# Sparse attention and two gated layers on one core: queries and keys of a pair of heads split once in half the columns and spread by transfers

## The chip, the cores and the metric

One core of a Trainium2 chip runs the whole program. The metric is the device time in microseconds of one execution; the kernel before was timed in three runs. Five engines work side by side, each through a queue of its own in a fixed order: TensorE (PE, matrix products into PSUM), VectorE (DVE), ScalarE (ACT), GpSimd (POOL) and SyncE (SP), which issues the transfers. GpSimd can't reach PSUM.

## What is computed

```python
def _attn_ref(q, k, v, tau):                     # each (4, 8, 576, 64)
    scores = scale * np.matmul(q, k.transpose(0, 1, 3, 2))
    thresh = np.max(scores, axis=-1, keepdims=True) - tau
    scores = np.where(scores >= thresh, scores, -1000000000.0)
    scores = scores - np.max(scores, axis=-1, keepdims=True)
    attn = np.exp(scores)
    attn = attn / (np.sum(attn, axis=-1, keepdims=True) + 1e-09)
    return np.matmul(attn, v)
x = attention, rearranged to (2304, 512)
x = (sigmoid(x @ w_gate) * (x @ w_val)) @ w_out  # inner width 1536
h = x @ w_in;  out = (h * cos(h)) @ w_out2       # inner width 2048
```

Everything is float32. The products run in a 32-bit format that keeps fewer bits, so each operand is split: a *high* part, rounded by a copy, and a *low* part, the value less the high part. A product is then made of high x high, high x low and low x high.

## The kernel before

There are 32 heads in 16 pairs (`Pair`, p = 0 to 15), four pairs to a batch. A pair has nine tiles of 128 query rows (`Queries`): four for each head's first 512 rows, and one (`h is None`) for the last 64 rows of both heads. A tile goes through PE (scores, L909, into one of two score banks `s`), DVE (row extreme, L915), ACT (exponent, L920), a threshold on ACT, DVE or POOL (L768 to L772), DVE (mask and sum, L923) and PE (transposes, L939 and L946). ACT then takes the high part of the transposed tile (L851) and its low part is made in one of three ways (`LOWS`, `LOWS_L`): by DVE (V, L862), by POOL from a copy of ACT's (G, L866 and L871), or by a product of PE's that subtracts the high part in the bank (T, L855 and L858). `Values` forms the products with the values (L1006), ACT and DVE add their halves into x32 (L976, L981), the row sums are inverted, sent through DRAM and spread (L1083, L1086), and x32 is scaled (L1097), split (L1115, L1119) and stored.

For a score, the 128 rows of a product hold the 64 columns of a head twice. `qh` holds the query highs in both halves of the rows, `ql` the query lows in both; `kk` holds the key highs in rows 0 to 63 and the key lows in rows 64 to 127. So qh x kk gives two of the terms and ql x kk the third (and a term low x low). For that, `Pair.load` fetches each of q and k twice, once into either half of the rows (two transfers of 64 rows; 1152 columns for q, 1216 for k, both heads side by side). Then the queries are scaled in place (letter s), the highs are taken (Q, J) and the lows (q on 128 rows, j on rows 64 to 127). `top_keys` and `last_queries` (letters k and d) copy what the tile of the last rows needs into `kh` and `qd`. The first pair is loaded and split in five pieces so that the first tile can start early (`begin` in `Pair.tasks`).

PE also runs a part of the feed-forward layer between attention's work: the gate and value products of batches 0 to 2 for three of the six column groups (letter P, L563 to L565, 144 groups of three matrices). A P needs the split x of two or four pairs of its batch. Their weights come as words that DVE shifts and joins (letters 4 and 5, L516 and L519; both operands in SBUF) before they are split.

Two things keep PE's clock up: 42 transposes of the identity into `warm` at the start (L597), and `filler` (letter D, L777), four transposes after certain scores (`FILL`), written into columns of the score bank that the scores leave free.

The order on each engine is written out by hand: one string for each engine in `ORDER`, a letter for each task, and which of the tasks with that letter comes next follows from the order in which they were made. `WHERE` names the engine of a pair's tasks (Q, q, J, j for queries and keys; Z, z for values; s for the scaling; X, x for the split of x; U for the scaling of x), `YS` that of a tile's threshold, `SHARED` the form of a value product. The rest of the program is put out after these strings and is ordered by `LATER` (L1877); PE goes from one to the other in its queue.

Of the kernel before, what the change touches and what calls it, by code (L numbers as in the profile page):

```python
# [9 lines left out]
F32 = mybir.dt.float32  # L10
# [45 lines left out]
        "SDDSTDSDDDDSTStNnTSNTSDtnDTTSNNNStTDNStTSTVDDtNSSTVBTtSSTTDDNtVSSTTVNNtSTVtSNnSTTNVtSNSBTtSNSTnVTTVNtSnSTTNN"  # L56
        "SNtPTPtPSSPVTTPSVPtSTPSBPPtTPSTSPTPStVPTTSSPVNtPNSPTSVtPTTPStVPTPBSPTtPSTPSTtPVSTTVtSSVTtVnSTTPSPtPTPPBSStPP"
        "TPSTSVtTPSPSTTVPtSPTSVtTVTStPSPPTBPStSTPVTTPSStVTPTPSPtSPTPStPVTTSVPtTPBSPStTPPTSPPTStVTPSStTVPSPSVTtVSPTTPP"
        "tSSTPBPtTSSTTVtPSTTVStSTtVnVTSTPStPTPBSPtTPSPTVSSTtVPSSTTPPtPTSPStPTVTSPtSTBPPTPVStSPTPSPTtPSVTTSVtSPTPSVPTt"
        "PSStTVBPTPSSTtPVTPSStTVPTTPSPTPtSPTPVSPttSPTPBSPTVStTVSTTPSPtVTPSStPPTtPSSPTVPTTSSVtPTPSBPTPtSSPTPTPStPSVTTV"  # L60
        "tSSTVtPTTVtPSBTPSPPTStPSTTVStVTPSTPPStPPTPStSVTPTSPtSTVPTBPSTtSPtVTPSSVTTVPStPTPtPPTPTPtVPBBVV"
    ),
    ACT=(
        "JQJQEQHwEYEHEhOEHo6HOEhowEHHHOOOYEhhHEO6hpwCEEHYH6hOsHEERwhCHaaHHYEhE6OFwEHCHHEOOh6hEYHFhpwOoEHYEOYHh6OEREHw"
        "aOhFHCoY6EEHHFahwOoEHHHOOOhhEEH6wehEeFHCEp6HEYehFHERwYYEChHeeEH6HehEYYEFHCwHEYeEHOhOFhp6eHEYhFwCYHeHEh6FHREe"
        "HEYheHCYEhHEXFeHEHHFhhEQHhEYpoaFHCHhEeEHeREEhYCHeHeEEhHCFEeHHEHFphheCHEhHFEHhFCEEYRHheeECHEHHeFhCEYYEFHHHeQE"
        "YYhhEeHhYpeFHHCEFZhECeHREYHChEHeeEChYHYEHFeEYYHEHFhheEFHhEpFECHHheHEREhHCeHEHhFYeEHEHFHhhJHhEYFEoHFpHCEhYHeR"
        "EhHeYEEHeFEEhHFCHHHEEYehhpeHEheEHHFhHCYEeEReCHFEHhYEHhECeEFCHHHEFhHphECEFHhCehHEEFCRHHYYEEhFCHeYhHEEHHHFXsHe"
        "hEhHEepFhhEHeRCEHeEFYhCHEHHFCEheYEFCHhhEEYHeheHHEYEeFpHHCEhFEHReEHCheEEHHeheEEFHCHHhhFpHEhFCHHYhEeRFCHEECHhE"
        "eeHCHFhEFEHHHEehhYeEHChEEYFHHephHEEFHCRHChhYEEHeFEFHCFHHEhhEHYhCpeHHXhFeFbFX"  # L70
    ),
    DVE=(
        "jqjMqKqMLMKKM4MKY5KMLYMK4KM5MKllKMlM4Y5KKIMMYlLYKK4lMML5KKlMM4KA5MlKlKAM4M5KKlMIMYKK45MMAzKLKAM4YKM5MllKKLMM"
        "Yl4KA5MKLIKMlAMLKK4lM5KLMMLlKKAMM4K5lKAMlMLlK4A5ILKlMALYMKLKlMMlKLKMALKLMLAllMKLxKAMLMIlKKLMMKKMlLMKKlMAMKYL"
        "LKLAllMIMKlLAKlMAYMKKLMMYlKKLMMlAKKALLMLMKllMLlKALIMKYAlKMMKzlKMLMlKKLMMAKLKLAllMMYYKALlMYAIKKLlMMLKKlMMLKLl"
        "AMKLKLLllAMMLKAKMLAIMlKLKMLlMYKKLMMAKKlAMMLLLKKllMLIMlYKKLLlAMMKKMYMKLlAKMlMKKMALLYKAlMMlYYIKKAlMMlLYKKAzMML"
        "KKlMMAlLKKLLLAxMLlMKLYlKMYAIllKMMKLMKYlAKMYLAMlKKAMMYllKKLlLMMYLKKAMMLYYIKAlLMKYKMMlYYKLKMLlMKKALLMllAILYlAK"
        "MLlKMAMKKMlMYYKLAMKlKAMLLMLllKKMMlKKLLMAMlLIYKKAMMllYKKLMMAAKLLMAllKKlULILxlxAUAAUxx"
    ),
    POOL=(  # L80
        "YZYzJYjs7cYQqYJ7jG7QqZYGz7YcYGJ7jsQ7YUqZY7XxcUXxYsYG7YQq7GJjY7GscQZGYzJ7qG7UjGYZzYcsxYUXqYYJGYjZYYGzYscQGJYG"
        "YqUZGjYXGczGsUXxxqGGYJGjscGQqZzJjUYXYGYGcYxZUYXxjGYsQzqYYYcsQYqGJZGYzjGsYcYGGUQZGqYGJGjUYcGXxZzYQqJYGUjGGcsZ"
        "XxGQqUXGxzJsGjYYcGQqGYGYGGYZcJjYzYUGZYGGzUYYcGGXXRR"
    ),
    SP=(
        "100W21kkdd0W21sWsssk0kWdd1ssssW0rrssssWdkk2RRdWssssrrWRRk0kWssss12ddgWgg0ddssssWrgg1sssrsWggRRgkDk0ssss2dgrr"
        "ssssRRgggk21kd0gssssDDgkr1rdgssssRg2dRkggssss0grgdrRRsgsssD2ggdg1kkssss0rDrdg2ssssg1gdRRggD2kkdssssrr1RRssss"
        "kggk0dssssggg1rr0sRsgss2dRggdkkDD0ssgrdsskkssssd2rggR1Rssssrr2g0Rksssggks1DddgRssssd0grr2ggRkssssdggRk10dggr"
        "ssDssrgssssggkgd1kR2ssgssRDggDdrssssdk2rRRkgssssggrrssssRRDDDDggg"
# [5 lines left out]
    "VTTVTTTGT VGVTGTTTT TGVTTTVGV VGVVGTVGV VVGVVVVGV VGVGVVGVG VGVGVVVVG GGVGVVVGV "  # L95
    "VGVVVVVVG VVVGVVVVV GGVGGVGGV GVGVVVVVG VGVGGVVGV VGVVGVVGV GGVGVVGVV VGGVGVGVV "
).replace(" ", "")
LOWS_L = (
    "TTVV VVTV TTVV VVVV VVTV VVVV VVVV VVVV VVTV VVVV VVVV VVVV VVVV VVVV VVVV VVVV "
# [10 lines left out]
    "SS.. S..S .... .... S... .... .... .... .... .... .... .... .... .... .... .... "  # L110
# [3 lines left out]
    Q="APPPPPAPAPPPPPPP", q="DPPPPPPPPPPPPPPP", J="APPPPPPPPPAPPPPP", j="DPPPPPPPPPPPPPPP",  # L114
    Z="PPPPPPPAPPPPPPPP", z="PPDPPPPDPPPDPPPP", s="APAPPPPPPPPPPAPP", X="PPAPPPPPPAPPPPAA", x="PPPDPPPPPDPPDDDD", U="PPPPPPPPPPPPPPDP",
)

YS = (
    "PPAPDDPAP DADDAPPPA AADPAPDPP DPAAAPAAA PAADAAPPP APPPAPPPD PPDADPAAA AADAPAAAA "
    "DDDPPPAPP AAPADPPPA PDAPDAPPD DDPDAAAPP DDPADDADA DADDDDDPP DAPPDDPAP PAPDADPPA "  # L120
).replace(" ", "")

BITS = "DDDDDDDDDDDD"

FILL = (
    "223002001 200002000 000000000 000000000 000000000 000000000 000000000 000000000 "
# [334 lines left out]
def tile_kernel(ctx: ExitStack, tc: tile.TileContext, q, k, v, tau, w_gate, w_val, w_out, w_in2, w_out2, out):  # L461
# [28 lines left out]
    def f32(ap):  # L490
        return ap.bitcast(F32)
# [99 lines left out]
    for t in (qhs[0][:, S:QW], qhs[1][:, S:QW], qds[0], qds[1]):  # L591
        nc.gpsimd.memset(f32(t), 0.0)
# [1347 lines left out]
```

## Time and profile before

| | us |
|---|---|
| median of 3 runs | 1111.09 |
| lowest, highest | 1110.85, 1112.88 |
| the profiled execution | 1111.66 |
| its span, first to last instruction | 1109.9 |
| PE busy | 1076.6 (97%) |
| DVE busy | 926.6 (83%) |
| ACT busy | 766.7 (69%) |
| POOL busy | 597.3 (54%) |
| first product of the feed-forward part (letter P) | at 84.96 |
| last attention product ends, `LATER` begins on PE | at about 401.7 |

Shares over the whole span mix stages. The attention stage ends near 402 us, and inside it the time before the first P and the time after it have to be read apart. A wait is put down to the operand that came last.

### The profile page before, as it was taken

The page shows a single profiled execution, that of the slowest core. Times are in us where ns is not written, and L with a number is a line of the kernel's source. Part 1 is how long each engine was busy: PE and PEld are TensorE (multiplying, and loading weights), DVE is VectorE, ACT ScalarE, POOL GpSimd, SP SyncE. Part 2 cuts the span into 40 slices and gives each one's busy share as a digit, 9 for nine tenths or more (in the row PEclk, how much of TensorE's full clock was granted, in tenths as well). Part 3 has the DMA queues.
Part 4 walks back from the last instruction along what each step waited for, and adds up shares of the span by engine and source line. Part 5 has one row for each costly group of instructions (what it writes and reads, how often), then busy time and mean ns, then how long its engine had stood idle before and what let it go on. Part 6 is the DMA issues. An engine that isn't in the chain of part 4 may idle for free.

```text
span 1109.9 us, 17653 instructions
## 1 busy us (share of the span) xinstructions
PE 1076.6 (97%) x5816; PEld 917.4 (83%) x5816; DVE 926.6 (83%) x1631; ACT 766.7 (69%) x1507; POOL 597.3 (54%) x508
## 2 busy tenths in 40 slices
PE   6889999999999999999999999999999999999998
PEld 6768888888888878987888888888888888888886
DVE  6999998998998856887887655879788899889997
ACT  5889879888888855555654434357876767797774
POOL 4788878878886625432234442244244525445563
PEclk9999999999999999999999999999999999999999
DMA  6657675766666449898876645685444445457752
GB/s 184 158 154 217 193 211 167 199 181 187 182 188 182 125 163 313 303 322 293 292 259 219 200 172 197 219 254 209 157 169 168 152 152 190 173 207 240 279 211 85
DMA packets 88093, 225.53 MB, mean 203 GB/s; under 512 B 14410, under 2 KB 22722, under 8 KB 78274
## 3 DMA queue, kind: packets, MB, share of 16 engines
q1 hardware_dynamic: 87842, 224.08, 63.1%
q8 instruction: 46, 0.75, 0.3%
q10 hardware_dynamic: 160, 0.33, 0.1%
q14 instruction: 45, 0.37, 0.1%
HBM read 150.18 MB, written 59.84 MB: 189 GB/s over the span
## 4 chain that ended last, share of the span: by engine, by line
PE 51%; DVE 1%; DMA 1%; ACT 0%; issue 0%; ACTq 0%
PE h L1391 5%; PE h L1392 5%; PE h L1393 5%; PE h L1580 4%; PE h L1581 4%; PE h L1582 4%; PE o L1700 4%; PE o L1701 4%; PE o L1702 4%; PE o L564 3%; PE o L563 3%; PE o L565 3%; DMA early<-gd 1%; PE o L1791 1%; PE o L1790 1%; PE o L1792 1%
## 5 line engine op out<-in xcount | busy, mean ns | idle before, releaser
L1626 POOL TENSOR_TENSOR g<-raws,g 128x512 fp32r<-128x512 f32 x68 | 94.6, 1400 | 138.1 <-ACT g L1625 115.9
L915 DVE TENSOR_REDUCE sm<-s 128x1 f32<-128x576 f32 x144 | 106.1, 750 | 10.9 <-PE s L909 8.1
L923 DVE SCALAR_TENSOR_TENSOR p<-s,sm,p 128x576 f32<-128x576 f32 x128 | 102.6, 812 | 12.0 <-ACT p L920 7.6
L920 ACT ACTIVATE p<-s,sm 128x576 f32<-128x576 f32 x128 | 94.0, 742 | 15.3 <-DVE sm L915 10.6
L1391 PE MATMUL h<-x,w 128*128 128x256 f32 (+1 forms) x304 | 101.4, 333 | 0.0
L1392 PE MATMUL h<-x,w 128*128 128x256 f32 (+1 forms) x304 | 101.3, 333 | 0.0
L1393 PE MATMUL h<-x,w 128*128 128x256 f32 (+1 forms) x304 | 101.3, 333 | 0.0
L851 ACT ACTIVATE PT<-t 128x512 fp32r<-128x512 f32 (+1 forms) x160 | 86.2, 554 | 21.6 <-PE t L939 18.1
L909 PE MATMUL s<-kk,qh 128*128 128x288 f32 x320 | 92.0, 318 | 9.3 <-DVE p L923 7.8
L1006 PE MATMUL v<-PT,vn 128*128 128x320 f32 (+2 forms) x532 | 84.8, 303 | 3.2 <-DVE x L981 3.2
L1710 DVE TENSOR_TENSOR y<-o,y 128x512 f32<-128x512 f32 x120 | 78.7, 682 | 6.1 <-PE o L1702 5.8
L939 PE MATMUL t<-ident,p 128*128 128x128 f32 x512 | 76.3, 276 | 3.5 <-DVE PT L862 1.9
L1006 PEld LDWEIGHTS v<-PT,vn 128*128 128x128 f32 (+1 forms) x532 | 74.0, 187 | 5.6 <-DVE x L981 4.1
L871 POOL TENSOR_TENSOR PT<-praw,PT 128x512 fp32r<-128x512 f32 x48 | 64.1, 1336 | 26.5 <-ACT praw L866 15.6
L1700 PE MATMUL o<-g,w 128*128 128x512 f32 x196 | 76.7, 392 | 0.5 <-ACT o L1716 0.5
L1701 PE MATMUL o<-g,w 128*128 128x512 f32 x196 | 76.4, 390 | 0.0
L1702 PE MATMUL o<-g,w 128*128 128x512 f32 x196 | 76.3, 389 | 0.0
L909 PEld LDWEIGHTS s<-kk,qh 128*128 128x128 f32 x320 | 58.8, 189 | 21.1 <-DVE p L923 9.9
L1580 PE MATMUL h<-form,w 128*128 128x512 f32 x192 | 75.0, 390 | 0.5 <-ACT side L1549 0.5
L1581 PE MATMUL h<-form,w 128*128 128x512 f32 x192 | 74.8, 389 | 0.0
L1582 PE MATMUL h<-form,w 128*128 128x512 f32 x192 | 74.7, 389 | 0.0
L528 POOL TENSOR_TENSOR w<-wt,w 128x512 fp32r<-128x512 f32 x30 | 39.6, 1325 | 64.5 <-ACT w L524 64.4
(207 smaller groups left out, 3520.2 us busy)
## 6 DMA issues: line engine op xcount, KB each, us to landing
w<-wd SPq DMA_DIRECT2D x62, 1024.0 KB
wd<-stage SPq DMA_DIRECT2D x64, 512.0 KB
gd<-st SPq DMA_DIRECT2D x64, 256.0 KB
wraw<-in_moe_w_out_dram SPq DMA_DIRECT2D x28, 512.0 KB
raw_k<-in_k_dram SPq DMA_DIRECT2D x30, 304.0 KB
raw_q<-in_q_dram SPq DMA_DIRECT2D x30, 288.0 KB
wraw<-in_moe_w_in_dram SPq DMA_DIRECT2D x16, 512.0 KB
spare<-gd SPq DMA_DIRECT2D x7, 1024.0 KB
```

The costliest lines, as they stand in the source:

```text
L909: nc.tensor.matmul(s[:, half, 0:HALF], qq, keys[:, half * HALF:half * HALF + HALF], start=(i == 0), stop=(i == len(mms) - 1),)
L915: nc.vector.tensor_reduce(self.sm()[:, 0:1], self.s()[:, :, 0:HALF], axis=AX.XY, op=ALU.min)
L1006: nc.tensor.matmul(o, w, x, start=z == 0, stop=z == len(steps) - 1)
L1391: nc.tensor.matmul(o, w_hi, x(0, c), start=begin, stop=False, **late)
L1392: nc.tensor.matmul(o, w_hi, x(1, c), start=False, stop=False, **late)
L1393: nc.tensor.matmul(o, w_lo, x(0, c), start=False, stop=c == KC - 1, **late)
L1580: nc.tensor.matmul(ps(), of(0, c), hi, start=fresh and c == 0, stop=False, skip_group_check=True)
L1581: nc.tensor.matmul(ps(), of(0, c), lo, start=False, stop=False, skip_group_check=True)
L1582: nc.tensor.matmul(ps(), of(1, c), hi, start=False, stop=c == 1, skip_group_check=True)
L1700: nc.tensor.matmul(ps(), of(0, c), hi, start=begin, stop=False, skip_group_check=True)
L1701: nc.tensor.matmul(ps(), of(0, c), lo, start=False, stop=False, skip_group_check=True)
L1702: nc.tensor.matmul(ps(), of(1, c), hi, start=False, stop=True, skip_group_check=True)
```

## The change

Queries and keys of a pair after the first are fetched once: the first head's columns in rows 0 to 63, the second's in rows 64 to 127, so 128 rows of 576 columns for q and 640 for k. They are scaled and split there, into `qsplit`, `ql`, `khi` and `klo`. Ten transfers then spread them: four copy the query highs of each head into both halves of the rows of `qh` (`both_rows`, letter u), four put key highs and lows into the halves of `kk` (`keys`, letter y), two put each head's query lows into its own rows of `qz` (`low_queries`, letter d). `qz` is zero in the other head's rows, so the third term is now qz x khi, with the key highs of both heads in the rows as they were split. The number and shape of PE's score products stay. `kh`, `qd` and their copies go.

The first pair keeps its five pieces; its inputs land in x32 and in `bc` instead of tiles of their own, and POOL copies its key highs (`first_keys`, a new task with the letter J), which all scores of the pair now await.

The warm transposes (9 groups instead of 14) go into `warm`, which takes its place in the ring of the output banks `v`; the first product with the values waits for them. The first ones are 36 instead of 42. At the start POOL zeroes 64 x 576 four times in `qz` and once in `khi`, instead of two `qd`.

All five strings of `ORDER`, and `LOWS`, `LOWS_L`, `SHARED`, `WHERE`, `YS` and `FILL` are new. Tasks by letter, before and after: POOL G 48, 51; POOL Y 55, 62; DVE Y 39, 53; ACT Y 50, 29; N 20, 18; n 7, 3; DVE l 89, 93; DVE z 3, 1; SP k 32, 0; d 32, 30; u 0, 60; y 0, 60. The products P, V, S and T are as many as before.

```diff
@@ ORDER and the tables @@
...
 FILL = (
-    "223002001 200002000 000000000 ...
+    "421001001 000000000 000000000 ...
@@ buffers @@
-    qls = [at.tile([P, 2 * QW], F32R, tag=f"ql_{i}", name=f"ql_{i}") for i in range(2)]
-    qds = [at.tile([P, P], F32R, tag=f"qd_{i}", name=f"qd_{i}") for i in range(2)]
-    for t in (qhs[0][:, S:QW], qhs[1][:, S:QW], qds[0], qds[1]):
-        nc.gpsimd.memset(f32(t), 0.0)
+    qlz = [at.tile([P, 2 * S], F32R, tag=f"ql_{i}", name=f"ql_{i}") for i in range(2)]
+    for i in range(2):
+        for t in (qhs[i][:, S:QW], qlz[i][64:128, 0:S], qlz[i][0:64, S:2 * S]):
+            nc.gpsimd.memset(f32(t), 0.0)
...
-    for _ in range(42):
+    for _ in range(36):
         nc.tensor.transpose(warm[:, 0:P], ident, ident)
@@ class Pair @@
+        def first_keys(self, part):
+            raw = self.first_raw("k", part)
+            moves = [(slice(64, P), SL, 0, S)]
+            if part.start == 0:
+                moves = [(slice(0, 64), SL, 0, S), (slice(0, 64), 0, SM, SL), (slice(64, P), 0, S, SL)]
+            for r, to, of, n in moves:
+                nc.gpsimd.tensor_scalar(self.khi()[r, to:to + n], raw[r, of:of + n], 1.0, 0.0, op0=ALU.mult, op1=ALU.add)
...
+        def both_rows(self, h, i):
+            nc.sync.dma_start(f32(self.qb()[64 * i:64 * i + 64, QW * h:QW * h + S]), f32(self.qh()[64 * h:64 * h + 64]))
+
+        def keys(self, h, i):
+            of = (self.khi, self.klo)[i]()[64 * h:64 * h + 64, SL * (1 - h):]
+            nc.sync.dma_start(f32(self.kb()[64 * i:64 * i + 64, S * h:S * h + S + SL * h]), f32(of))
+
+        def low_queries(self, h):
+            r = slice(64 * h, 64 * h + 64)
+            nc.sync.dma_start(f32(self.qz()[r, S * h:S * h + S]), f32(self.ql()[r]))
...
+        def whole(self):
...
+            for nm, load, high, low, n in (("q", "0", "Q", "q", S), ("k", "1", "J", "j", S + SL)):
...
+            dup = [[task("SP", 0.47, "u", lambda h=h, i=i: self.both_rows(h, i), qh, uses=[self.qh, self.qb], moved=S // 2)
+                    for i in range(2)] for h in range(2)]
+            kks = [[task("SP", 0.47, "y", lambda h=h, i=i: self.keys(h, i), (kh, kl)[i], uses=[(self.khi, self.klo)[i], self.kb],
+                         moved=S // 2) for i in range(2)] for h in range(2)]
+            low = [task("SP", 0.47, "d", lambda h=h: self.low_queries(h), ql, uses=[self.qz, self.ql], moved=S // 2) for h in range(2)]
+            return [[*dup[h], *kks[h], low[h]] for h in range(2)], []
...
-    def filler(s):
+    spare = buf("v", lambda: warm, 2, any_order=True)
+    fills = []
+
+    def filler():
 
         for _ in range(4):
-            nc.tensor.transpose(s()[:, 1, HALF:HALF + P], ident, ident)
+            nc.tensor.transpose(spare()[:, 0:P], ident, ident)
@@ scores @@
             if h is None:
-                mms = [(pair.qb()[0][:, q0:q0 + P], kk[:, k0:k0 + S]) for q0, k0 in ((SM, 0), (S + SL, S + SL))]
-                mms.append((pair.qd(), pair.kh()))
+                mms = [(pair.qb()[:, q0:q0 + P], kk[:, k0:k0 + S]) for q0, k0 in ((SM, 0), (S + SL, S + SL))]
+                mms.append((pair.qz()[:, SM:SM + P], khi[:, SL:SL + S]))
             else:
-                q0 = (QW + SL) * h + P * self.j
-                mms = [(qq[:, q0:q0 + P], kk[:, S * h:S * h + S]) for qq in pair.qb()]
+                q0 = P * self.j
+                mms = [(pair.qb()[:, (QW + SL) * h + q0:(QW + SL) * h + q0 + P], kk[:, S * h:S * h + S]),
+                       (pair.qz()[:, (S + SL) * h + q0:(S + SL) * h + q0 + P], khi[:, SL * (1 - h):SL * (1 - h) + S])]
```

## Rows read from the trace of the kernel before

**Rows 1.** Page: busy us and share of the span of each engine

```profile
PE 1076.6 (97%) x5816; PEld 917.4 (83%) x5816; DVE 926.6 (83%) x1631; ACT 766.7 (69%) x1507; POOL 597.3 (54%) x508
```

**Rows 2.** Stretches: length, busy us by engine, granted clock, DMA share, GB/s

```profile
20.00:85.00 65.00, 52.70 (x345) 44.33 (x343) 60.76 (x110) 53.68 (x121) 54.09 (x47) 0.97 0.60 157
85.00:402.00 317.00, 309.27 (x2010) 270.89 (x2009) 287.75 (x640) 266.09 (x591) 248.74 (x234) 1.00 0.64 179
402.00:1110.00 708.00, 700.37 (x3372) 589.32 (x3370) 568.24 (x864) 438.12 (x782) 288.06 (x212) 1.00 0.63 219
```

**Rows 3.** Timeline of PE, first P: start, duration, engine, line, operation

```profile
84.96 0.48 PE L563 MATMUL m<-xs_a,w 128*128 128x512 f32 x1
```

**Rows 4.** Groups of POOL, 0 to 402 us: count | busy us, mean ns | idle before

```profile
L685 POOL TENSOR_TENSOR kk<-raw_k,kk 64x1216 fp32r<-64x1216 f32 x15 | 42.1, 2804 | 1.2
L685 POOL TENSOR_TENSOR ql<-raw_q,qh 128x1152 fp32r<-128x1152 f32 x15 | 40.8, 2717 | 0.6
...
L1097 POOL TENSOR_TENSOR x<-x,bc 128x576 f32<-128x576 f32 x14 | 20.0, 1426 | 2.8 <-DVE x L981 2.7
...
L670 POOL TENSOR_SCALAR kk<-raw_k 128x1216 fp32r<-128x1216 f32 x14 | 17.0, 1215 | 0.0
```

**Rows 5.** Timeline of DVE: shifts of weight words, held and free

```profile
22.06 2.12 DVE L519 SCALAR_TENSOR_TENSOR wt<-we,wt 128x512 uint32<-128x512 uint32 x1
...
27.86 0.42 DVE L516 TENSOR_SCALAR wt<-wraw 128x512 uint32<-128x512 uint32 x1
...
37.50 2.72 DVE L516 TENSOR_SCALAR wt<-wraw 128x512 uint32<-128x512 uint32 x1
...
57.54 0.67 DVE L519 SCALAR_TENSOR_TENSOR wt<-we,wt 128x512 uint32<-128x512 uint32 x1
...
117.85 2.02 DVE L516 TENSOR_SCALAR wt<-wraw 128x512 uint32<-128x512 uint32 x1
```

**Rows 6.** Timeline of POOL at the same time

```profile
37.15 2.79 POOL L685 TENSOR_TENSOR kk<-raw_k,kk 64x1216 fp32r<-64x1216 f32 x1
```

**Rows 7.** Groups of DVE, 0 to 402 us

```profile
L862 DVE TENSOR_TENSOR PT<-t,PT 128x512 fp32r<-128x512 f32 x68 | 46.4, 685 | 3.3 <-ACT PT L851 2.6
...
L1119 DVE TENSOR_TENSOR xs_a<-x,xs_a 128x512 fp32r<-128x512 f32 x4 | 6.3, 1583 | 0.0
L685 DVE TENSOR_TENSOR vn<-raw_v,vn 128x640 fp32r<-128x640 f32 x3 | 4.2, 1412 | 0.1
```

**Rows 8.** Waits of DVE, 0 to 20 us: waiter, released by: us, times, longest

```profile
DVE p L923 <- PE s L777: 1.5, 1, 1.5
...
DVE sm L915 <- PE s L777: 1.3, 1, 1.3
```

**Rows 9.** Timeline, the start

```profile
1.36 6.81 PE L597 MATMUL warm<-ident 128*128 128x128 f32 x42 [1.36 <-POOL halfpi L476]
...
5.15 0.74 ACT L668 ACTIVATE kk<-raw_k 128x640 fp32r<-128x640 f32 x1 [1.70 <-DMA raw_k<-in_k_dram]
...
7.92 0.38 PE L909 MATMUL s<-kk,qh 128*128 128x288 f32 x1
```

**Rows 10.** Timeline of PE; a stretch, columns of rows 2

```profile
42.69 0.40 PE L909 MATMUL s<-kk,qh 128*128 128x288 f32 x1 [2.40 <-DVE p L923]
...
44.00:48.00 4.00, 4.00 (x27) 3.96 (x25) 3.33 (x9) 2.36 (x5) 3.48 (x2) 0.69 0.80 196
```

**Rows 11.** DMA issues, one issue on SP's timeline, and a wait of SP's queue

```profile
kh<-kk SPq DMA_DIRECT2D x32, 144.0 KB
...
33.90 0.59 SPq L689 DMA_DIRECT2D kh<-kk  x1
...
SPq L1086 <- DMA rd<-rs: 5.2, 5, 1.8
```

**Rows 12.** Timeline: query lows of the second pair, its first scores

```profile
30.05 2.64 POOL L685 TENSOR_TENSOR ql<-raw_q,qh 128x1152 fp32r<-128x1152 f32 x1
...
34.80 0.37 PE L909 MATMUL s<-kk,qh 128*128 128x288 f32 x1 [0.96 <-DVE p L923]
```

More of the change, by code (lines that the diff above doesn't have):

```diff
@@ L640, in queries, with load @@
-        def queries(self, to, part):
-            n, head = part.stop - part.start, part.start // S
-            if n <= S:
-                begin = part.start + (QW - S) * head
-                return to[:, begin:begin + n]
-            return to.rearrange("p (a n) -> p a n", a=2)[:, :, 0:S]
-        def as_queries(self, part):
-            raw = self.raw["q"][:, part]
-            return raw if part.stop - part.start <= S else raw.rearrange("p (a n) -> p a n", a=2)
-        def scaled(self, part, engine):
-            raw = self.raw["q"][:, part]
+        def load(self, nm, part=None, queue=nc.sync):
+            src = self.src[nm][self.p]
+            if nm == "v" or self.p:
+                self.raw[nm] = at.tile([P, src.shape[1]], F32, tag=f"raw_{nm}", name=f"raw_{nm}")
+                queue.dma_start(self.raw[nm], src)
+                return
+            src = self.src[nm][NP].rearrange("(d a) n -> d (a n)", a=2)
+            for i in range(2):
+                queue.dma_start(self.first_raw(nm, part)[64 * i:64 * i + 64], src[:, part])
@@ L708, in tasks @@
-            order = [(nm, i) for i in range(2) for nm in "qkv" if i < len(parts[nm])]
-            if begin:
-                order = [("q", 0), ("k", 0), ("q", 2), ("k", 1), ("q", 1), ("v", 0)]
-                nc.sync.dma_start(taus[:, 0:1], tau.to_broadcast([P, 1]))
-                self.load("q", parts["q"][0])
-                self.load("k", parts["k"][0], nc.scalar)
-                nc.scalar.activation(one, halfpi, AF.Exp)
-                nc.vector.tensor_scalar(factor_q, taus[:, 0:1], 0.0, scale, op0=ALU.is_ge, op1=ALU.mult)
-                nc.vector.tensor_scalar(off, taus[:, 0:1], 0.0, None, op0=ALU.max)
@@ L753, in tasks @@
+            self.vb = buf("vn", size=2)
+            of, rest = self.whole() if p else self.begin()
             self.scores = {(h, j): of[h] + rest * (j > 0 and h == 0) for h in range(2) for j in range(4)}
-            self.scores[None, None] = of[0] + of[1] + rest + keys + last_q
+            self.scores[None, None] = of[0] + of[1] + rest
     N = NP * NT
@@ L959, in __init__ @@
             pv = task("PE", products(n, (14 if self.shared else 9) + self.close), "V", self.product, *pair.ready[blk, h],
[L960 removed]
+                      *lasts, pair.v_done, pvs[0], *(fills if pvs[0] is None else []), uses=[bank, self.PT, self.LZ, pair.vb])
             pvs[0] = pv
@@ L1887, in _two @@
     t = a.reshape(NP, 2, S, D).transpose(0, 1, 3, 2)
-    parts = [t[:, 0], t[:, 1, :, SM:], t[:, 1, :, :SM]] + [t[:, 1, :, SM:]] * again
-    return _np.concatenate(parts, axis=2)
+    last, most = t[..., SM:], t[..., :SM]
+    both = _np.concatenate([last, most, last], axis=3)
+    heads = [both[:, 0, :, 0 if again else SL:], both[:, 1, :, :S + again * SL]]
+    whole = _np.concatenate(heads, axis=1)
+    first = _np.concatenate([t[0, 0], both[0, 1, :, :S + again * SL], t[0, 0, :, :again * SL]], axis=1)
+    return _np.concatenate([whole, first.reshape(1, P, -1)], axis=0)
 def _values(a):
```

255 lines of the change are left out of this document (140 added, 115 removed).

## The prediction

> **What bounds the kernel now.** I read the page first, then the same engines by stretches, then the idle times of each engine with what ended them. The page shows TensorE (PE) busy for 97% of the span and VectorE (DVE) for 83% [rows 1]; that is an average over stages. Cut in three, it separates [rows 2]. From 20 to 85 us PE is busy 52.7 of 65 us and DVE 60.8: DVE sets the pace, ScalarE and GpSimd (53.7 and 54.1) are close behind. At 84.96 the first gate product of the feed-forward part starts [rows 3]; it is the work that fills PE's gaps, and it cannot start before two pairs of heads of batch 0 are finished and split. From 85 to 402 us PE is busy 309.3 of 317 us; from 402 on 700.4 of 708. So the end is set by two things in series: how soon the first pairs get through DVE, and then PE's own work. An edit that shortens DVE's way before 85 us moves all that follows. An edit on GpSimd or ScalarE counts only through that, and after 85 us there are 7.7 us of PE's idle time to win in all.
>
> The change sits in that frame. It touches the preparation of queries and keys (GpSimd work nearly throughout), the warm transposes, and every order. Nothing after 402 us is changed; that stage keeps its length.
>
> **Sum, step by step.** The profiled execution took 1111.66 us for a span of 1109.9; the median of the three is 1111.09, 0.6 lower. I sum against 1111.66 and take the 0.6 off at the end.
>
> *The split in half the columns.* Before, a pair after the first costs GpSimd 2.72 us for the query lows and 2.80 us for the key lows, and three one-input copies (scale, query highs, key highs) of about 1.2 us each (40 on GpSimd in all, of which one group stands) [rows 4]: 9.2 us. After it the lows have 576 and 640 columns: 1.43 us, which is what a two-input operation of 576 columns takes [rows 4], and 2.80 x 640/1216 = 1.48; the copies halve to 0.6. That is 4.7 us a pair, 4.5 less, some 67 us over 15 pairs, of which about 14 go back to GpSimd in the new division of work (three more 512-column lows, seven more thresholds, value lows). GpSimd is not the engine that is late, so none of this is a gain by itself.
>
> What it does for DVE is. DVE operations whose operands all lie in SBUF stop while GpSimd runs. The shifts of the weight words take 0.42 and 0.67 us when free; the one at 37.50 took 2.72, because GpSimd's key lows ran from 37.15 to 39.94 [rows 5, 6]. Seven of them were held by a 2.7 or 2.8 us operation, the first at 22.06 and the last at 117.85 [rows 5]; together they lost 11.9 us, the five before 85 us 8.9 us. With operations half as long (1.45/2.76 = 0.53) and as many meetings the five lose 4.7, a gain of 4.2; if the chance of a meeting halves too, they lose 2.5, a gain of 6.4. I take 4.8, near the cautious end, since GpSimd gets other work in place. The two after 85 us (2.9 us) help only where PE waits: 0 to 1.5, I take 0.5.
>
> *What DVE gets instead.* I counted the letters of the old and new order lines of DVE up to the 36th row maximum (four pairs). The new one has three more 512-column lows at 0.685, two lows of x at 1.58, one value low less at 1.41 [rows 7], and small ones (two low strips more, two sums and a masking not yet reached) that cancel these down by about 1.4: 2.1 + 3.2 - 1.4 - 1.4 = 2.5 us more. Below, this may be 0, since the two x lows end on DVE sooner than behind GpSimd's queue and let the first products start earlier; above, the count up to the 45th maximum gives 5.8. I take +2.5. ScalarE has some 6 us less up to the same place and PE some 5 (warm transposes, and the subtractions by PE that were turned into lows on DVE); DVE covers both, so I put them at 0. If DVE were not late they would be worth up to those figures.
>
> *Warm transposes in a bank of their own.* Before, they write into the score bank, so the readers of the scores wait for them: DVE waited 1.3 and 1.5 us on them near the start [rows 8]. These waits go: 0 (another operand is late then) to -2.8. I take -1.5, because scores, maximum, exponent and mask form a chain in the first 20 us and no other engine covers it. There are 9 groups instead of 14. They now share the ring of the output banks, and the first output product waits for them; it needs the masks and transposes of the same tiles and comes later than they do, and that covers them.
>
> *Start.* The 42 first transposes run from 1.36 to 8.17 and the first scores at 7.92 come out of the same queue behind them [rows 9]. Six fewer give PE back 0.9 us. Against that the first scores now also need the keys copied by GpSimd: about 700 columns, at the rate of the 1216-column copy 0.7 us, after some 3100 columns of memsets at no more than that rate (3.1 us from 1.3 on). They start when the keys have landed, which is where ScalarE's copy starts at 5.15 [rows 9], and end near 5.9, beside the highs and lows of the same keys and before the 7.92. Without that cover, 0.7 us. I take 0; the ends are -0.9 and +0.7.
>
> *The clock.* After 2.40 us of idle PE before 42.69, which ended with a mask on DVE queued behind the held shifts, the granted clock falls; in 44 to 48 us it is 0.69 [rows 10], a mixture of 2.4 and 1.2 GHz, which takes 1.2 us of full speed from PE. A shorter hold makes that idle shorter; fewer warm transposes make another fall likelier. I take -0.7, with ends -1.2 and +1.2.
>
> *Transfers.* A pair now has two loads of 128 rows in place of four of 64 rows and twice the columns, and ten copies between SBUF rows in place of four: 60 for the query highs, 60 for the keys, 30 for the query lows, each of 64 rows and 144 to 160 KB like the one that they replace [rows 11]. By shape that is 22 MB of copies more, 4.7 and 9 MB of old copies and loads less: 8 MB net in 402 us, 21 GB/s on the 179 and 0.64 share of the DMA engines [rows 2], so a share near 0.72. SyncE issues one in 0.59 us [rows 11]. Queued ahead of use they cost nothing: the last of a pair's copies is issued up to 5 x 0.59 = 3 us after the split, and a transfer that depended on another waited 1.0 us on average and 1.8 at the longest [rows 11]. So 4 to 4.8 us are added behind a split that is 4.5 shorter, and the earlier start on GpSimd covers it. I take 0.
>
> The Trainium skill speaks against this edit: "SBUF — State Buffer", section "The DMA setup-cost knee", gives each transfer about 2 us whatever its size and asks for 128 rows and few large transfers, and the section before it says that 64 rows reach only half of the ports. By its figures one such copy is an estimated 2 + 147/218, or 2.7 us, and the copies of a pair would land 0.9 to 1.7 us later than by the rows. No row of this trace shows one transfer alone.
>
> Sum: -4.8 - 0.5 + 2.5 - 1.5 + 0 - 0.7 + 0 = -5.0, so 1106.7 for an execution like the profiled one and **1106.1 us** for the median. All good ends together give -12.8 (6.4, 1.5, 2.8, 0.9, 1.2), 1098.3; the bad ends 4.2 - 5.8 - 0.7 - 1.2 make +3.5, 1114.6, before any late transfer.
>
> **Rivals.** *Late transfers, slower.* The scores of a pair stand in PE's queue and wait for five copies that stand in SyncE's queue behind stores that themselves wait. For it: the old preparation is already just in time; the first query lows of the second pair end at 32.69 and its scores start at 34.80, 2.1 us later [rows 12]. Against it: GpSimd has more than 4 us a pair to begin sooner. The gain of 5.0 is gone at 0.33 us of waiting for each of 15 pairs; at 0.6 us it is 9 - 5 = +4, about 1115. The rule quoted above is this rival's.
>
> *Nothing to measure.* DVE stays 93% busy from 20 to 85 us, gets more lows and thresholds, and the time that it no longer loses to GpSimd is spent by other waits of an order written for a model. The 2.5 and 5.8 of added work against 4.2 to 4.8 of saved holds leave -0.5 or so: 1110.5. For it speaks that PE's 7.7 us after 85 are out of reach either way.
>
> *GpSimd was late as well, larger gain.* PE has 12.3 us idle from 20 to 85 us. If the freed GpSimd lets the pairs be prepared early enough that the first products begin 8 us sooner, and starts and warm transposes give 2.5 more, it is 1100. Against it speaks that DVE's idle time in that stretch is 4.2 us.
>
> **How the numbers follow.** About 0.2% (2.2 us) is what a measurement can tell from no change. The forecast, faster within 1102 to 1108.8, gets 0.50; the larger gain 0.12; nothing to measure 0.20; late transfers, or the clock falling again, 0.18. So faster 0.62, same 0.20, slower 0.18. The range goes from 1100 to 1113: below it lies half of the larger gain, above it most of the slower case.
>
> **What would show it.** In the profile after: no shift of the weight words near 2.7 us, and few above 1.5; no wait of DVE or ScalarE on a warm transpose; GpSimd some 50 us less busy up to 400 us; the first gate product 4 to 6 us before 84.96 and the stretch from it to the last attention product as long as before, 317 us. It is wrong if scores show waits on the copies, if the first product is no earlier, if the granted clock shows more low stretches, or if the stretch after the first product gets shorter, which would mean that it was not PE's own work.

## The result, and the profile after

| | before | after |
|---|---|---|
| median, us (4 runs each, side by side) | 1111.99 | 1091.93 |
| lowest, highest of after | | 1091.60, 1094.26 |
| profiled execution, us | 1111.66 | 1094.26 |
| first product of the feed-forward part (P) | 84.96 | 70.84 |
| last attention product ends | 401.7 | 384.95 |

The ratio of after to before is 0.9824, with a 95% interval of 0.9805 to 0.9843: 20 us faster, where 5 were forecast; 1091.9 lies below the range of 1100 to 1113. The profiled execution happens to be the highest of its four, so the traces have 17.4 of the 20 us to explain; the other 2.7 stand in no trace.

The first line is the page's busy time by engine of the kernel after, against [rows 1]:

```profile
PE 1071.8 (98%) x5784; PEld 912.5 (84%) x5784; DVE 909.9 (83%) x1647; ACT 764.4 (70%) x1488; POOL 543.7 (50%) x521
```

GpSimd is 53.6 us less busy; DVE is 16.7 us less busy although it has 16 instructions more. The stretches of the kernel after, cut at its own first P and at the end of attention (columns of [rows 2]):

```profile
0.00:70.84 70.84, 61.19 (x410) 53.05 (x410) 61.33 (x133) 59.59 (x127) 51.68 (x72) 1.00 0.79 215
...
70.84:384.95 314.11, 309.66 (x2005) 269.86 (x2003) 280.13 (x651) 266.06 (x581) 205.68 (x238) 1.00 0.74 206
384.95:1092.50 707.55, 700.95 (x3373) 589.62 (x3372) 568.45 (x864) 438.71 (x782) 286.35 (x212) 1.00 0.63 218
```

Before [rows 2, 3] the three lengths were 84.96, 316.7 and 708.2 us. So 14.1 us are gained ahead of the first P, 2.6 between it and the end of attention, and 0.6 behind. In the middle stretch PE is as busy as before (309.7 against 309.3); only its idle time shrank, from 7.7 to 4.5. The granted clock is 1.00 in all three; the stretch at 0.69 of [rows 10] is gone.

For the first stretch the same view of the kernel before, up to its own first P:

```profile
0.00:84.96 84.96, 66.95 (x438) 57.17 (x439) 70.58 (x128) 62.48 (x135) 60.47 (x63) 0.98 0.62 163
```

DVE, which sets the pace here, was busy for 70.58 us and idle for 14.38 (84.96 less 70.58). After, it is busy for 61.33 and idle for 9.51. The 14.1 us are thus 9.2 of busy time and 4.9 of idle time, and the runs below show a cause of its own for each. The shifts of the weight words in the same stretch, as groups of DVE (count | busy us, mean ns | idle before), before and then after:

```profile
L519 DVE SCALAR_TENSOR_TENSOR wt<-we,wt 128x512 uint32<-128x512 uint32 x8 | 12.9, 1607 | 0.1
L516 DVE TENSOR_SCALAR wt<-wraw 128x512 uint32<-128x512 uint32 x8 | 8.0, 1000 | 0.0
```

```profile
L520 DVE SCALAR_TENSOR_TENSOR wt<-we,wt 128x512 uint32<-128x512 uint32 x7 | 6.0, 863 | 0.0
L517 DVE TENSOR_SCALAR wt<-wraw 128x512 uint32<-128x512 uint32 x7 | 3.2, 450 | 0.0
```

At the free durations of [rows 5], 0.67 and 0.42 us, the sixteen of before should take 8.7 us and took 20.9: 12.2 us were lost to holds. The fourteen of after should take 7.6 and took 9.2: 1.6 lost. So the holds gave 10.6 us, two shifts that moved behind the first P gave 1.1, and all other work of DVE grew from 49.7 to 52.1 us, by 2.4: -10.6 - 1.1 + 2.4 = -9.3. With the idle time (-4.9), the stretch behind the first P (-2.6) and the last one (-0.6) that makes the 17.4 us.

### The profile page after: what moved, and what is told of

It is laid out like the page before. It is cut to its first block, busy times and chain, and to the rows that moved or that the text cites. A ratio compares the mean times of both kernels' runs of the same rounds, so it can differ in the third digit from the quotient of the medians.

```text
span 1092.5 us, 17726 instructions
## 1 busy us (share of the span) xinstructions
PE 1071.8 (98%) x5784; PEld 912.5 (84%) x5784; DVE 909.9 (83%) x1647; ACT 764.4 (70%) x1488; POOL 543.7 (50%) x521
## 2 busy tenths in 40 slices
DMA packets 94494, 234.06 MB, mean 214 GB/s; under 512 B 13258, under 2 KB 21570, under 8 KB 84674
## 4 chain that ended last, share of the span: by engine, by line
PE 51%; DVE 2%; DMA 1%; ACT 1%; issue 0%; ACTq 0%
PE h L1441 5%; PE h L1442 5%; PE h L1443 5%; PE h L1630 4%; PE h L1631 4%; PE h L1632 4%; PE o L1750 4%; PE o L1751 4%; PE o L1752 4%; PE o L565 3%; PE o L566 3%; PE o L564 3%; DMA early<-gd 1%; PE o L1840 1%; PE o L1842 1%; PE o L1841 1%
## 5 line engine op out<-in xcount | busy, mean ns | idle before, releaser
L1056 PE MATMUL v<-PT,vn 128*128 128x256 f32 (+3 forms) x532 | 84.7, 302 | 0.2 <-ACT st L1214 0.2
L919 POOL TENSOR_TENSOR PT<-praw,PT 128x512 fp32r<-128x512 f32 x51 | 66.7, 1307 | 35.4 <-ACT praw L914 16.9
L959 PE MATMUL s<-khi,ql 128*128 128x288 f32 x288 | 81.0, 295 | 0.6 <-DVE ql L670 0.6
L1675 ACT ACTIVATE g<-raws 128x512 fp32r<-128x512 f32 x106 | 64.3, 624 | 13.1 <-DVE raws L1718 8.3
```

The costliest lines, as they stand in the source:

```text
L959: nc.tensor.matmul(s[:, half, 0:HALF], qq, keys[:, half * HALF:half * HALF + HALF], start=(i == 0), stop=(i == len(mms) - 1),)
L1056: nc.tensor.matmul(o, w, x, start=z == 0, stop=z == len(steps) - 1)
```

## Shorter lows and an own bank, each alone in the old order

Three kernels keep the old split and the old strings. In the first, GpSimd takes the query and key lows of every pair after the first on half the columns only; half of these lows are left out, and besides that only one memset is added at the start.

```diff
+                if self.p and engine == "POOL":
+                    part = slice(0, S)          # queries
...
+                if self.p and engine == "POOL":
+                    part = slice(0, S + SL)     # keys
```

> The kernel before, strings and all, but GpSimd's query and key lows of pairs 1 to 15 compute half of their columns (1152 to 576, 1216 to 640); the other half of the lows is left out, so the scores lack terms. Lighter GpSimd is enough (no new order needed): the shifts lose 4 to 6 us to GpSimd in place of 16.6, first gate product near 77, 1100 to 1105 us. Order needed as well: the time stays within 1107 to 1112 us, because what stands behind each operation in the old strings still comes at its old place.

Measured: 1101.78 us against 1111.71, ratio 0.9907 (0.9888 to 0.9927), 9.9 us faster. Its first stretch, then one shift and the key lows that hold it (timelines of DVE and GpSimd: start, duration):

```profile
0.00:79.66 79.66, 65.72 (x439) 56.14 (x439) 65.12 (x128) 62.20 (x135) 53.59 (x64) 1.00 0.67 174
```

```profile
36.53 1.50 DVE L516 TENSOR_SCALAR wt<-wraw 128x512 uint32<-128x512 uint32 x1
```

```profile
36.18 1.57 POOL L689 TENSOR_TENSOR kk<-raw_k,kk 64x640 fp32r<-64x640 f32 x1
```

It is the shift that took 2.72 us in [rows 5]. Then it ended 0.28 us behind the GpSimd operation of [rows 6] (40.22 and 39.94); now it ends 0.28 us behind one that is about half as long (38.03 and 37.75). DVE runs the same 128 instructions in 65.12 us instead of 70.58, and its idle time stays, 14.54 against 14.38. So shorter lows act on DVE's busy time alone. A GpSimd that was late is not the way as far as the waits show: up to 402 us of the kernel before, DVE and PE's products wait for GpSimd only at the very start (1.3 and 1.4 us). The shifts lose 6.2 us instead of 12.2 before the first P, which comes 5.3 us sooner; attention ends 8.8 us sooner (392.87), so 3.5 more are won behind the first P, where the shifts up to 200 us lose 1.2 us instead of 4.5. The clock is 1.00 in 44 to 48 us here too. In the kernel before it was down shortly ahead of that and into it (columns of [rows 2]):

```profile
43.00:46.50 3.50, 3.50 (x18) 3.44 (x17) 2.56 (x8) 2.21 (x4) 2.90 (x3) 0.51 0.94 242
```

So the 9.9 us include whatever that cost, at most 1.7 us of PE's work.

Not every meeting holds the shift. At 57.54 us [rows 5] it took its free 0.67 us in the kernel before, and GpSimd's operation at that moment was the longer one, with 2.11 us where its group has a mean of 1.34:

```profile
57.25 2.11 POOL L871 TENSOR_TENSOR PT<-praw,PT 128x512 fp32r<-128x512 f32 x1 [0.39 <-ACT praw L866]
```

In the second, the kernel before gets the own bank for its warm transposes and nothing else; only the ten groups that come before the first product with the values stay.

```diff
-    "223002001 200002000 000000000 ...
+    "223002001 000000000 000000000 ...
...
-            nc.tensor.transpose(s()[:, 1, HALF:HALF + P], ident, ident)
+            nc.tensor.transpose(spare()[:, 0:P], ident, ident)
```

> The kernel before, its warm transposes in a bank of their own; of the 14 later groups the four that stand behind the first product with the values are left out (the bank is handed on by then). The changed kernel lost 4.5 us when its groups went back to the score bank. If the bank is worth that in any order: 1106 to 1108 us, the waits on the warm transposes in the first 20 us gone, first gate product near 81. If it is worth it only where the new order made room: 1110 to 1112; slower if the four groups that are missing let the clock fall.

Measured: 1107.10 us against 1110.61, ratio 0.9966 (0.9955 to 0.9977), 3.5 us faster. First P at 81.51:

```profile
0.00:81.51 81.51, 65.12 (x423) 55.02 (x423) 70.42 (x128) 62.30 (x135) 60.18 (x63) 0.98 0.66 170
```

Now the busy time stays (70.42 against 70.58) and the idle time falls from 14.38 to 11.09. The bank acts on DVE's idle time alone. The four groups that are left out have no part in it: they stood on PE behind the first product with the values, at 37.22 us in the kernel before, and the 3.45 us by which the first P comes sooner are there by 31 us (the same shift, before and then with the own bank):

```profile
30.77 2.48 DVE L519 SCALAR_TENSOR_TENSOR wt<-we,wt 128x512 uint32<-128x512 uint32 x1
```

```profile
27.32 2.92 DVE L498 SCALAR_TENSOR_TENSOR wt<-we,wt 128x512 uint32<-128x512 uint32 x1
```

What went is more than DVE's two waits of [rows 8]. In the first 20 us of the kernel before, ScalarE's exponent waited longer for the warm transposes, and they for DVE (us, times, longest):

```profile
ACT p L920 <- PE s L777: 3.7, 3, 1.8
...
PE s L777 <- DVE sm L915: 2.3, 3, 0.9
```

The third has both, and the scaling and the query highs on half the columns as well (these halves are left out).

```diff
+            part = slice(0, S)                  # scaling
...
+                if self.p:
+                    part = slice(0, S)          # query highs
```

> The kernel before, strings and all, with both: warm transposes in their own bank (the same ten groups) and GpSimd's and ScalarE's scaling, query highs, query lows and key lows of pairs 1 to 15 on half of the columns (the other half is left out, so the scores are wrong); key highs stay whole. No copies. That takes 4.0 of the 4.5 us a pair off GpSimd that the change takes off. If the gain is the lighter split and the bank, and the strings only follow it: 1093 to 1098 us. If the new strings carry a share of their own: 1100 us or more.

Measured: 1097.09 us against 1110.61, ratio 0.9880 (0.9865 to 0.9895), 13.5 us faster: the sum of the two, 9.9 + 3.5.

```profile
0.00:75.04 75.04, 64.17 (x423) 54.70 (x423) 64.12 (x128) 60.97 (x135) 52.09 (x65) 1.00 0.71 184
```

Busy 64.12, idle 10.92: both effects at once. The two add up, which leaves little for the shorter copies. From here to the kernel after 5 to 6 us are left (5.2 by the medians, 6.2 by the ratios). In the timelines up to 200 us, 9 of this kernel's 24 shifts are still held by a GpSimd operation (by over 0.15 us), and lose 6.6 us by it: query and key lows, but also a value low, probability lows (`PT`, L871 in the kernel before) and the scaling of x, which no split shortens. None of the nine is held mainly by a copy of key highs, the one operation that this kernel leaves long.

## The own bank in the new order

The kernel after with its warm transposes back in the score bank (the eighth of the nine groups goes with the ninth tile's scores instead of the sixth's).

```diff
-            nc.tensor.transpose(spare()[:, 0:P], ident, ident)
+            nc.tensor.transpose(s()[:, 1, HALF:HALF + P], ident, ident)
```

> The changed kernel with its nine later groups of warm transposes written into the score bank again, as before (one group of the sixth tile is moved to the ninth). If the bank of their own is worth what my prediction took, about 1.5 us, and at most 2.8: 1093 to 1095 us, DVE or ScalarE wait 2 to 5 us on them in the first 20 us. If it is worth nothing: 1092.

Measured: 1096.46 us against 1111.71, ratio 0.9868 (0.9849 to 0.9887): 4.5 us of the gain are gone, more than the 1 to 3 expected. Its stretches and its waits from 0 to 20 us (us, times, longest; L822 is the warm transpose there):

```profile
0.00:20.00 20.00, 14.96 (x85) 13.57 (x86) 8.16 (x16) 9.14 (x15) 9.37 (x23) 0.91 0.58 164
20.00:75.57 55.57, 47.74 (x326) 40.66 (x325) 52.39 (x118) 50.36 (x112) 42.82 (x49) 1.00 0.81 216
```

```profile
ACT PT L896 <- PE t L986: 3.3, 1, 3.3
DVE p L970 <- PE s L822: 2.9, 3, 1.3
...
PE s L822 <- DVE p L970: 2.0, 2, 1.0
...
ACT p L967 <- PE s L822: 1.6, 1, 1.6
```

Up to its first P DVE is busy for 60.55 us (after: 61.33) and idle for 15.02 (after: 9.51). Again only the idle time. The waits are not DVE's alone: ScalarE's exponent waits for the warm transposes, and the transposes, queued on PE behind the scores whose bank is in use, wait for DVE and ScalarE in turn. That is a ring through three engines, and pricing DVE's share of it gave too little. The clock of 0.91 in the first 20 us, where after has 1.00, has a share in the 4.5 us that this run doesn't divide from that of the waits.

## How much room GpSimd has in the new order

Three kernels change only the length of GpSimd's query and key lows in the kernel after. One writes each low twice in a single operation of 1152 or 1280 columns; one does it in two operations of 576 or 640; both do all the work, and some of it twice. The third takes half of the columns and leaves the other half out.

```diff
+            if nm != "v" and engine == "POOL":                         # one long operation
+                n = S if nm == "q" else S + SL
+                to = low_raw[nm].rearrange("p (a n) -> p a n", a=2)
+                raw, hi = (t.unsqueeze(1).to_broadcast([P, 2, n]) for t in (raw, f32(hi)))
+                eng.tensor_tensor(to, raw, hi, op=ALU.subtract)
+                return
             eng.tensor_tensor(to, raw, f32(hi), op=ALU.subtract)
```

> The changed kernel, but GpSimd's query and key lows of pairs 1 to 15 compute their columns twice in one instruction (2.8 and 3.1 us in place of 1.4 and 1.6; the second result lands on the raw input, which nobody reads again). Everything else as it was. Short operations: DVE is held again, shifts above 1 us on average, first gate product at 76 to 80, 1098 to 1104 us. Order: the strings place the shifts away from the lows, shifts stay below 0.8, at most 1094 us.

```diff
             eng.tensor_tensor(to, raw, f32(hi), op=ALU.subtract)
+            if nm != "v" and engine == "POOL":                         # two short ones
+                eng.tensor_tensor(raw.bitcast(F32R), raw, f32(hi), op=ALU.subtract)
```

> As the run with long lows, but the second result comes from a second instruction of the same size, so GpSimd has the same work in short pieces. Short operations: DVE can go between the two, so shifts stay near those of the changed kernel (0.44 and 0.78 us) and the time within 1092 to 1095 us. GpSimd late (its load counts, not the length of an instruction): the same time as with long lows, 1098 or more.

```diff
+            if nm != "v" and engine == "POOL":
+                n = (S if nm == "q" else S + SL) // 2
+                raw, hi, to = raw[:, 0:n], hi[:, 0:n], to[:, 0:n]
```

> The changed kernel with GpSimd's query and key lows of pairs 1 to 15 on half of their columns (288 and 320; the rest is left out). GpSimd still late in the new strings (doubled lows cost 20 us): 1085 to 1089 us. GpSimd has room now and PE's own work sets the pace from the first gate product on: within 1.5 us of 1092.

Measured: one long operation 1111.89 us against 1110.93, ratio 1.0013 (1.0002 to 1.0024); two short ones 1116.51, ratio 1.0050 (1.0033 to 1.0067); half 1089.24 against 1110.61, ratio 0.9806 (0.9792 to 0.9821). So the long lows give back all 20 us, far more than expected, and short ones of the same sum still more; halving the lows again brings only 2.7 us.

The waits of DVE that tell it are those for a threshold of GpSimd, up to 385 us in after and half, up to 450 in the other two (the order of the fences: after, long, two, half):

```profile
DVE p L973 <- POOL sm L815: 2.5, 3, 1.3
```

```profile
DVE p L984 <- POOL sm L826: 11.8, 12, 2.1
```

```profile
DVE p L980 <- POOL sm L822: 15.0, 13, 2.6
```

```profile
DVE p L980 <- POOL sm L822: 0.7, 2, 0.4
```

With one long operation the first P comes at 77.07, 6.2 us later than in after, and the shifts before it lose 7.6 us instead of 1.6: that is the hold. DVE's busy time grows by 5.6 of the 6.2 us there (66.97 against 61.33), of the threshold waits only 0.4 us fall there, and the granted clock of 0.96 can have cost no more than the rest. From there to the end of attention it takes 325.5 us instead of 314.1, 11.4 more, and there stand the threshold waits, 11.4 of the 11.8 us. PE's scores wait for those masks in turn, here up to 460 us in after and with one long operation:

```profile
PE s L959 <- DVE p L973: 2.5, 6, 0.7
```

```profile
PE s L970 <- DVE p L984: 13.5, 14, 2.3
```

So a long low does two things: it holds a shift, and it stands ahead of a threshold in GpSimd's queue, for which DVE's mask waits. Two short operations hold the shifts less (3.5 us lost before the first P) and delay the thresholds more; their first P comes at 75.93 with a granted clock of 0.93 before it. What of their longer time the clock costs, and what the waits, these runs do not divide.

## The split and the order apart

Can the order be had without the split, or the split without the order? The first kernel puts the old split under the new strings and tables, with the own bank (a few neighbouring letters exchanged where an operand had no buffer yet; `kh` gets a second buffer).

```diff
-ORDER, LOWS, LOWS_L, SHARED, WHERE, YS, FILL of before
+those of after; on SP no u, and k for the last two of each four y
```

> Queries and keys are split as before (full width, no spreading copies but those for the last tile), under the strings and tables of the changed kernel, with its 36 first and 9 later warm transposes in their own bank; SyncE's string has the spreading copies taken out, six tasks of pair 13 stand a few places later, and kh has two buffers. Short operations (the gain is DVE no longer held by 2.7 and 2.8 us operations of GpSimd): the holds come back, shifts of the weight words near 1.1 and 1.4 us, 1103 to 1110 us. Order (the strings and tables bring the gain, whatever the split): 1092 to 1097 us. Both needed: in between, near 1100.

Measured: 1156.28 us against 1110.93, ratio 1.0406 (1.0387 to 1.0425), 45 us slower than before, where 1092 to 1110 was expected. One wait of DVE and one of PE, up to 450 us:

```profile
DVE p L926 <- POOL sm L770: 31.0, 15, 8.4
```

```profile
PE s L912 <- DVE p L926: 18.5, 21, 2.8
```

The new strings hand GpSimd seven thresholds more, and behind the long split DVE's masks wait up to 8.4 us for one. In the kernel before no mask waits for a threshold of GpSimd.

The second puts the new split under the old strings and tables with warm transposes in the score bank, SyncE's order left to the program's planner; the third takes the new string for SyncE.

```diff
-ORDER, LOWS, LOWS_L, SHARED, WHERE, YS, FILL of after
+those of before, with JJ ahead on POOL; SP planned (second) or the string of after (third)
```

> The new split and its copies under the strings and tables of before, with 42 first transposes and 14 groups in the score bank; SyncE's tasks stand in the order in which the program's own model finds them ready. Short operations: shifts below 0.8 us on average, first gate product near 72, 1095 to 1100 us. Order: shifts still held about half as long as before, 1105 to 1111 us; slower than before if the copies come late in an order that has no room for them.

> As the run of the new split under the old strings, but SyncE follows the changed kernel's string (six of its tasks and one of ScalarE's stand a few places later). If the first such run was slow only because its SyncE string was bad at the start (the first weights came 7 us late): 1100 to 1107 us, first gate product near 78. If the old strings of the compute engines don't fit the new split: 1110 or more.

Measured: 1123.84 us against 1110.93, ratio 1.0117 (1.0097 to 1.0137), and 1226.67 against 1111.71, ratio 1.1039 (1.1017 to 1.1062). Waits of PE in the second:

```profile
PE t L896 <- ACT PT L892: 10.6, 4, 8.6
...
PE s L952 <- DMA qh<-qsplit: 1.8, 1, 1.8
```

And one of DVE, up to the first P:

```profile
DVE wt L513 <- DMA wraw<-in_moe_w_gate_dram: 7.0, 1, 7.0
```

The holds fall (the shifts up to 200 us lose 4.1 instead of 16.6), yet the time grows: DVE is busy for only 61.67 of the 97.33 us up to the first P, and 7.0 us of its idle time are one wait for the weights, whose load the planned order of SyncE brings late. The third shows only that a string of SyncE that fits no other string costs far more than the change is worth. Neither part alone is a gain as it stands in the change, copies and all: old and old 1111, old split and new order 1156, new split and old order 1124, new and new 1092. What the split takes off GpSimd is a gain in the old order too, as the half lows show; what costs more under the old strings these waits tell only in part.

## The copies

The first of two kernels issues each of a pair's ten copies twice in a row, to the same place; the second sends a further copy of the same rows to places of their own in DRAM, 150 transfers more.

```diff
+            for _ in range(2):
                 nc.sync.dma_start(f32(self.qb()[...]), f32(self.qh()[64 * h:64 * h + 64]))
```

> The changed kernel with each of the 150 spreading copies issued twice in a row (150 more transfers, 22 MB more, some 80 us more of SyncE's queue). Copies are hidden with room to spare: within 1 us of 1092. Copies are nearly late already (the rival of late transfers): scores wait for them, 1096 us or more.

```diff
+            nc.sync.dma_start(junk[self.p, 2 * h + i, :, 0:S], f32(self.qh()[64 * h:64 * h + 64]))
```

> The changed kernel with a second transfer behind each of the 150 spreading copies that takes the same rows to a place of its own in DRAM, so that it waits for none (in the run with doubled copies each second copy waited some 2.4 us in SyncE's queue for the first one to the same place). Copies hidden with room in DMA and in SyncE's queue: within 2 us of 1092. The DMA engines or SyncE's queue nearly full: 1097 us or more, with waits of PE on copies.

Measured: 1473.26 us against 1111.71, ratio 1.3255 (1.3229 to 1.3280), and 1167.87 against 1110.61, ratio 1.0514 (1.0494 to 1.0533). The first did not load the transfers as meant: the second copy waits in SyncE's queue until the first has landed, and all behind it waits too. That wait measures a copy. Waits of SyncE's queue:

```profile
SPq L714 <- DMA qh<-qsplit: 146.6, 60, 4.7
...
SPq L724 <- DMA ql<-ql: 73.3, 30, 4.4
SPq L719 <- DMA kk<-khi: 73.0, 30, 5.1
SPq L719 <- DMA kk<-klo: 67.3, 30, 4.0
```

360.2 us over 150 copies: 2.4 us from the end of an issue to the landing, at most 5.1. In the second nothing waits so; waits of SyncE up to 460 us are replaced by issues back to back, here on its timeline:

```profile
34.57 0.77 SPq L714 DMA_DIRECT2D qh<-qsplit  x1
35.38 0.71 SPq L715 DMA_DIRECT2D junk<-qsplit  x1
36.18 0.62 SPq L714 DMA_DIRECT2D qh<-qsplit  x1
36.84 0.69 SPq L715 DMA_DIRECT2D junk<-qsplit  x1
```

```profile
POOL raw_q L691 <- DMA raw_q<-in_q_dram: 20.6, 6, 7.7
POOL vn L706 <- DMA raw_v<-in_v_dram: 17.8, 5, 6.0
...
PE s L963 <- DMA kk<-klo: 8.4, 4, 2.8
```

Summed over SyncE's timeline (an issue together with the short gap to the next of its kind), after has 480 issues that fill 298 us of the 385 up to the end of attention, before 421 that fill 277 of 402; with the extra copies it is 630 that fill 407 of 459. Loads of the next pairs, queued behind the copies, then come late, and with them the split. In after PE, DVE and ScalarE wait for no copy at all, and GpSimd once, for 1.4 us. So the copies are hidden, but SyncE is 77% filled, 89% with the extra copies, and 150 transfers more cost 76 us. They also load the DMA engines (share 0.80 between the first P and the end of attention, 0.74 in after); the run doesn't divide the two.

## Why the prediction was wrong

**The frame held in the main.** The end is set by the first P and then by PE's own work: 14.1 of the 17.4 us lie ahead of the first P, and the stage behind attention kept its length to 0.6 us. No shift is near 2.7 us (the longest up to 200 us is 1.34), no wait on a warm transpose is left, and GpSimd is 53.6 us less busy, 51.9 of them before attention's end. But the first P is 14.1 us earlier, not 4 to 6, and the stretch behind it is 2.6 us shorter than the 317 us that it was to keep. The prediction named that as a sign of being wrong: PE's work there is the same, and the gain came out of the 7.7 us of idle time, of which its sum had taken 0.5.

**The held shifts, -4.8 and -0.5: the step that failed most.** The mechanism was right, and so was the halving: in the old order the shorter lows took 6.0 us of holds off before the first P, inside the 4.2 to 6.4 given, all of it at the five shifts that the sum named (8.9 us lost there before, 2.9 then). Two things around it were wrong. First, "as many meetings" was taken over to an order written anew. In after, 3 of the 24 shifts up to 200 us are held by over 0.15 us, in before 15; so the loss before the first P fell from 12.2 to 1.6, by 10.6 and not by 4.8. The sum counted seven meetings with query and key lows, 11.9 us, and left the other eight out. One of these, in the trace of before:

```profile
40.33 1.57 DVE L519 SCALAR_TENSOR_TENSOR wt<-we,wt 128x512 uint32<-128x512 uint32 x1
```

```profile
40.02 1.33 POOL L871 TENSOR_TENSOR PT<-praw,PT 128x512 fp32r<-128x512 f32 x1
```

GpSimd has three such probability lows more in after, and no shift is held by one: that points to the strings, since the old order with light splits still loses 4.6 us before its first P where after loses 1.6. Second, the two shifts after 85 us were put at 0.5, at most 1.5, because they help only where PE waits; the half lows in the old order won 3.5 behind the first P, and after won 2.6. Both lie within PE's 7.7 us of idle time, but above the bound of 1.5.

**Added work on DVE, +2.5:** 2.4 measured, shifts set aside, but in part by luck. The 2.4 are up to the first P, which comes behind the 26th row maximum in both kernels; the count went to the 36th, and up to there the other work grew by 0.9 (69.1 to 70.0 us). And the largest entry was wrong, two lows of x at 1.58 us each:

```profile
L1169 DVE TENSOR_TENSOR xs_a<-x,xs_a 128x512 fp32r<-128x512 f32 x2 | 1.4, 684 | 0.0
```

They took 0.68. The 1.58 was the mean of a group of which a member took up to 2.73 us and another 0.67, a mean with holds in it. Letters can be counted; their price has to be that of the free operation.

**The own bank, -1.5 within 0 to -2.8:** 3.5 in the old order and 4.5 in the new one. The step that failed is the bound: it was DVE's two waits of [rows 8] and left out that ScalarE's exponent waits for the same transposes (3.7 us), and PE's transposes for the bank (2.3 us). The cost of a shared bank is the whole ring's.

**The start, 0:** the first row maximum is at 8.6 us instead of 8.7. **The clock, -0.7:** the low stretch went, here and with the half lows alone. In 43.0 to 46.5 us of the kernel before the granted clock was 0.51, which takes 1.7 us of full speed from PE; the 1.2 of the sum were for 44 to 48 us, which cuts off its start. It is part of the 14.1.

**The transfers, 0:** right on the result; the DMA share is 0.79 before the first P and 0.74 behind it, where 0.72 was expected, and the traffic grew by 8.5 MB for the whole program (234.06 against 225.53), where 8 were worked out. But the price of one copy was too low: 2.4 us behind its issue in the run with doubled copies, not 1.0 to 1.8. So it is not because they are short that they are hidden. That the loads and splits run far enough ahead, as the sum had it, fits, but no run moves them alone.

The Trainium skill, "SBUF — State Buffer", section "The DMA setup-cost knee", was quoted against the change with about 2 us a transfer, an estimated 2.7 us for one such copy. The 2.4 us lie nearer to its figure than to that of the rows, but no product waited for a copy, so the loss that the prediction drew from it did not come.

**The rival "GpSimd was late as well"** named the size best (1100) but not the mechanism: in before no mask and no score product waits for GpSimd, so an earlier preparation was not what was missing. What it cost was DVE's time, through the holds. "Against it speaks that DVE's idle time is 4.2 us" overlooked that a held operation counts as busy: of the 70.58 us that DVE was busy before the first P, 12.2 were waiting. Only in the new order is GpSimd's queue itself without room, as the lows of twice the work show.

**What stays open:** what lies between the light kernel in the old order (1097.1) and after (1091.9). DVE's account to the first P gives 2.8 us busy and 1.4 idle, and the holds alone 3.0; that the new strings bring this is read from the traces, not from a run that changes them alone, since the strings of one split don't fit the other.

## What to carry to other kernels

An engine that shows 93% busy may be waiting inside its instructions: compare each group's mean with its shortest member, sum the excess over the stretch that sets the pace, and look up what runs on the other engine at that moment; that sum, not the idle time, shows what the other engine's shorter work can bring. An order is written for the durations and transfers that it had: the shorter lows alone gained 9.9 us in the old order, but the split with its copies cost 13 to 115 us under the old strings, and the new strings cost 45 with the old split. Price a shared buffer by all engines that pass through it, not by the waits of the one that sets the pace.

## What the runs showed of the hardware

- A DVE shift with its operands in SBUF that is held by a running GpSimd operation ends about 0.28 us (L516) or 0.55 us (L519) behind it, in all held shifts of the kernel before up to 200 us: 2.72 us with key lows, 1.57 with a probability low, 0.85 with a value copy, 1.50 with key lows of half the columns; free it takes 0.42 or 0.67. The profile counts the hold as busy time. At 57.54 us it was GpSimd's operation that took longer, 2.11 us where the mean is 1.34.
- A transfer of 64 rows and 144 to 160 KB between SBUF rows landed 2.4 us after its issue on average, 5.1 at most (doubled copies). A second one to the same place, which this program has wait for the first, held up the whole queue for that time: 360 us of such waits, in a kernel that took 381 us longer.
- SyncE takes about 0.55 us for an issue (the median up to the end of attention), and 0.62 to 0.77 in the run of issues without a gap that is shown for the extra copies. At 480 issues in 385 us the queue itself is a resource to be counted, like an engine.
